# Pooled keys of the first batch on TensorE, and 768 instead of 1408 columns of zeros

## The chip, the cores and the metric

One core of a Trainium2 chip. The metric is the device time of one execution in microseconds. A core has five engines that run beside each other: TensorE (PE; its weight loads are listed as PEld), VectorE (DVE), ScalarE (ACT), GpSimd (POOL) and SyncE (SP), which issues the transfers (DMA).

## The reference, cut to what matters

The input is q, k and v of 2 batches, 8 heads, 576 positions and 64 elements a head, in f32. Two attentions are added. One is local (a position sees those nearer than 4), the other pooled: q, k and v are averaged over groups of 4 positions, attended over 144 positions, and each row of the result is repeated 4 times.

```
q_d = q.reshape(B, H, Sd, 4, D).mean(axis=3)      # k_d, v_d alike
out_up = np.repeat(sm_attn(q_d, k_d, v_d), 4, axis=2)
out_local = softmax(where(|i - j| < 4, scale * q k^T, -1e9)) v
x = out_up + out_local                            # to (1152, 512)
h = max(x @ w_in, 0);  x = (s * h * h + b) @ w_out         # 512 -> 2048 -> 512
out = sum over e of p[:, e] * (max(x @ w1[e], 0) @ w2[e])  # 4 experts, 512 -> 1024 -> 512
```

## The kernel before, in words

The attention comes in 16 units: four groups (a batch, and the first or second half of its positions) of four pairs of heads. Units 0 to 3 and 8 to 11 are first halves; only these load k and the pooled v of their pair, and the second half uses what they left. Eight loop steps (`steps`) take a unit through `a_step` (L484: k and q are transposed on TensorE and copied out by ScalarE), `k_step` (L534: on GpSimd, the transposed keys kT are added in groups of four, with two additions, tk and kd), `b_step` (L551: mask, local scores, pooled scores from kd, maxima and exponentials), `norm_step`, `c_step` (p is transposed), `d_step` (products with v), `x_step` and `v_step` (pooled v, on GpSimd). A loop turn i gives each step the unit i minus the step's lag, so the units overlap.

A planner orders the instructions of each engine by their priority and its own estimate of time; `a_step` and `b_step` of the first four units have a raised priority. GpSimd alone keeps the order in which the loop writes it. Every engine then runs its list in order. SP issues all the loads of q, k, v and weights in one list.

Matmuls on a tile of zeros (`idle`) fill TensorE's list: eight of 512 columns at the start, and at five places of a unit. `keep_warm` (L358) takes the free columns of the bank that the place has just written, and repeats a matmul of so many columns until the number in `fill` is reached; in `b_step` there are `fill // 448` of them ahead of the scores. `fill` is 1408 for units 0 to 3, 512 for units 4 to 9 and 0 after. ScalarE's copy out of a bank waits for the filler in it.

From loop turn 2 the weights of the first layer are prepared: they are split in a high and a low f32 part by ScalarE (L157, L196) and VectorE (L161 to L199). Partial products of the first layer (`ahead_products`, L761) start in the attention; they hold banks of the pool `psm`, which has three, and open a bank with one matmul on zeros (L771). After the attention come the rest of the first layer and the experts.

Of the kernel before, what the change touches and what calls it, by code (L numbers as in the profile page):

```python
# [8 lines left out]
F32 = mybir.dt.float32  # L9
# [3 lines left out]
ACTF = mybir.ActivationFunctionType  # L13
ALU = mybir.AluOpType
# [8 lines left out]
def attn_moe_moe_kernel(  # L23
# [14 lines left out]
    nc = tc.nc  # L38
# [4 lines left out]
    P = 128  # L43
# [7 lines left out]
    FAC = 4  # L51
    SD = S // FAC
    ND = SD // 2
    KP = 96
    KR = S // KP
    NP = H // 2
# [3 lines left out]
    scale = 1.0 / float(D) ** 0.5  # L60
    NEG = -8.0e9

    const = ctx.enter_context(tc.tile_pool(name="const", bufs=1))
# [5 lines left out]
    psm = ctx.enter_context(tc.tile_pool(name="psm", bufs=3, space=bass.MemoryType.PSUM))  # L69
# [255 lines left out]
        nc.vector.tensor_copy(identb[:, a], ident[:TQ, :TQ])  # L325

    mask = const.tile([TQ, MX + 2, W], BF16, name="mask")

    def make_mask(t, m):
        if t == 0:  # L330
            nc.gpsimd.memset(mask, 0.0)
        off = t * TQ - window(t) if t <= MX else S - TQ - window(NTQ - 1)
        for sgn in (1, -1):
            nc.gpsimd.affine_select(
                out=mask[:, t : t + m],
                in_=mask[:, t : t + m],
                compare_op=ALU.is_ge,
                fill=NEG,
                base=FAC - 1 + sgn * off,
                pattern=[[0, m], [-sgn, W]],  # L340
                channel_multiplier=sgn,
            )
# [15 lines left out]
    def keep_warm(ps, c0, cols):  # L358
        n = 512 - c0
        for _ in range(-(-cols // n) if n > 64 else 0):  # L360
            nc.tensor.matmul(ps[:, c0:], idle[:, :P], idle[:, :n], start=True, stop=True)  # L361
# [20 lines left out]
    NU = NG * NP  # L382
    actx = ExitStack()
    ap1 = actx.enter_context(tc.tile_pool(name="att1", bufs=1))
# [3 lines left out]
    psa = actx.enter_context(tc.tile_pool(name="psa", bufs=5, space=bass.MemoryType.PSUM))  # L388
    loaded = {}
    st = {}  # L390
    fill = [1408 if u < NP else 512 if u < 2 * NP + 2 else 0 for u in range(NU)]
    sums = [const.tile([P, MX + 2, 1], F32, name=f"sum{i}") for i in range(2)]

    GB = CUT * TQ // FAC
# [3 lines left out]
    def unit(u):  # L398
        g, j = divmod(u, NP)
        b, hf = divmod(g, HALVES)  # L400
        return g, j, b, hf

    def tiles(hf):

        return (0, CUT) if hf == 0 else (CUT, NTQ - CUT)
# [6 lines left out]
    def bank():  # L412
        return psa.tile([P, 512], F32, tag="a", name="psa")
# [70 lines left out]
    def a_step(u):  # L484
        g, j, b, hf = unit(u)
        if hf == 0:
            kn = loaded.pop(("k", u))
            kT = ap1.tile([P, S], F32, tag=f"kT{j}", name=f"kT{j}")
            view = kT.rearrange("p (n r) -> p n r", r=KR)
            m = KR // 2  # L490
            for c in range(2):
                psk = bank()
                for i in range(m):
                    last_pe["att"] = nc.tensor.transpose(
                        psk[:, i * KP : i * KP + KP],
                        kn[:, c * m + i].rearrange("p a d -> p (a d)"),
                        ident[:KP, :KP],
                    )
                keep_warm(psk, m * KP, fill[u])
                nc.scalar.activation(  # L500
                    out=view[:, :, c * m : c * m + m],
                    in_=psk[:, : m * KP].rearrange("p (t n) -> p n t", n=KP),
                    func=ACTF.Copy,
                    scale=scale / (FAC * FAC),
                )
            st["kT", j] = kT
        qn = loaded.pop(("q", u))
        n0, m = tiles(hf)
        gd = m * TQ // FAC
        psq = bank()  # L510
        for r in range(FAC):
            last_pe["att"] = nc.tensor.transpose(  # L512
                psq[:, r * gd : r * gd + gd],
                qn[:gd, r].rearrange("p a d -> p (a d)"),
                ident[:gd, :gd],
            )
        keep_warm(psq, m * TQ, fill[u])
        qz = ap2.tile([P, MX * TQ], F32, tag="qz", name="qz")[:, : m * TQ]
        nc.scalar.activation(
            out=qz.rearrange("p (t n r) -> p t n r", t=m, r=FAC),  # L520
            in_=psq[:, : m * TQ].rearrange("p (r t n) -> p t n r", r=FAC, t=m),
            func=ACTF.Copy,
            scale=float(FAC * FAC),
        )
        qd = ap2.tile([P, MX * TQ // FAC], F32, tag="qd", name="qd")[:, :gd]
        nc.vector.tensor_reduce(
            out=qd,
            in_=psq[:, : m * TQ].rearrange("p (r n) -> p n r", r=FAC),
            axis=AX.X,
            op=ALU.add,  # L530
        )
        st["q", u] = qz, qd

    def k_step(u):  # L534
        g, j, b, hf = unit(u)
        if hf == 0:
            kv = st["kT", j].rearrange("p (n r) -> p n r", r=FAC)
            t = ap4.tile([P, SD, 2], F32, tag="tk", name="tk")
            nc.gpsimd.tensor_tensor(out=t, in0=kv[:, :, :2], in1=kv[:, :, 2:], op=ALU.add)
            kd = ap1.tile([P, SD], F32, tag=f"kd{j}", name=f"kd{j}")  # L540
            nc.gpsimd.tensor_tensor(out=kd, in0=t[:, :, 0], in1=t[:, :, 1], op=ALU.add)
            st["kd", j] = kd
# [458 lines left out]
    def side_step():  # L1001
# [15 lines left out]
    steps = [  # L1017
        (b_step, 1),
        (a_step, 0),
        (k_step, 0),  # L1020
        (d_step, 3),
        (c_step, 2),
# [7 lines left out]
    for i in range(last + 1):  # L1030
# [13 lines left out]
        for f, lag in steps:  # L1044
            u = i - lag
            if 0 <= u < NU:

                with tc.high_priority(ahead.get(f, 0)) if f in ahead and u < NP else nullcontext():
                    f(u)
            if f is x_step and u >= 0 and u % NP == NP - 1:  # L1050
                slots += l1_steps(0, u // NP) + l2_steps(0, u // NP)
                firsts.append(slots[-FC - KD])
                if u < NP:

                    for _ in range(3):
                        take_slot()
            if f is norm_step:
                for g, (wait, n_fc) in AHEAD.items():
                    for kk in range(KD - 1):
                        if g * NP + kk + 3 + wait <= i < g * NP + NP + 3:  # L1060
                            for fc in range(n_fc):
                                if (0, 0, fc // 2) in ready:
                                    ahead_products(g, kk, fc)
            if f in (k_step, c_step) and slots and i < last:
                take_slot()
            if f in (b_step, k_step, c_step, v_step):
                side_step()
            if 5 <= i <= 7 and f in (d_step, norm_step):
                side_step()
# [112 lines left out]
```

## Time and profile before

| | us |
|---|---|
| median of 3 runs | 683.9 (683.66 to 684.03) |
| the profiled execution | 683.63 |
| its span | 681.9 |
| TensorE busy | 673.8 |
| VectorE busy | 403.9 |
| ScalarE busy | 344.5 |
| GpSimd busy | 104.2 |

Busy times are sums over the span; what bounds a stage is read from the chain of waits and from tables of that stage. The records of matmuls overlap in time, as they are pipelined: the chain gives how far one after another moves the work on, a line's mean the length of one record.

### The profile page before, as it was taken

How to read it: one execution, taken by the hardware profiler on the slowest of the kernel's cores; microseconds unless marked ns; L12 is line 12 of the kernel's file. 1: busy time of each engine (PE TensorE's matmuls, PEld its weight loads, DVE VectorE, ACT ScalarE, POOL GpSimd, SP SyncE). 2: the span in 40 equal slices, each digit the busy share in tenths (PEclk: the TensorE clock that was granted, in tenths of full speed). 3: DMA queues.
4: the chain of work that ended last, by engine and by line, in shares of the span. 5: the costliest groups of instructions: out<-in, count | busy, mean ns of one | idle time of the engine just before them, and what ended most of it. 6: DMA issues, size and time to landing. Idle time of an engine off the chain costs nothing.

```text
span 681.9 us, 11959 instructions
## 1 busy us (share of the span) xinstructions
PE 673.8 (99%) x4790; PEld 614.2 (90%) x4790; DVE 403.9 (59%) x720; ACT 344.5 (51%) x846; POOL 104.2 (15%) x123
## 2 busy tenths in 40 slices
PE   9999999999999999999999999999999999999997
PEld 6778888999999999999999898898998999989996
DVE  2899867798934325695435645546456365455442
ACT  3778688788856657754544333334234233333320
POOL 4431541100002001021201200211112012010000
PEclk9999999999999999999999999999999999999999
DMA  9986944234400001000301201111102012110012
GB/s 185 221 187 121 151 125 134 77 124 135 176 0 1 32 1 62 1 32 1 93 3 61 62 31 45 50 32 62 31 32 67 28 38 86 31 33 31 1 62 77
DMA packets 54167, 46.43 MB, mean 68 GB/s; under 512 B 32224, under 2 KB 42720, under 8 KB 54112
## 3 DMA queue, kind: packets, MB, share of 16 engines
q1 hardware_dynamic: 54112, 45.67, 25.3%
q8 instruction: 37, 0.61, 0.4%
q14 instruction: 18, 0.15, 0.1%
HBM read 43.31 MB, written 2.36 MB: 67 GB/s over the span
## 4 chain that ended last, share of the span: by engine, by line
PE 87%; DVE 7%; ACT 4%; POOL 1%; issue 1%; POOLq 0%; ACTq 0%; DVEq 0%
PE psm L316 40%; PE psx L902 26%; PE psx L316 13%; PE psa L361 2%; ACT pl L571 1%; PE psa L591 1%; PE psa L657 1%; PE psm L775 1%; PE psa L512 1%; DVE pl L632 1%; DVE cv L186 1%; DVE cv L175 1%; PE psa L685 0%; DVE cv L161 0%; DVE h L812 0%
## 5 line engine op out<-in xcount | busy, mean ns | idle before, releaser
L316 PE MATMUL psm<-w,h 128*128 128x512 f32 x864 | 208.7, 391 | 0.0
L316 PEld LDWEIGHTS psm<-w,h 128*128 128x128 f32 x864 | 158.5, 188 | 30.0
L902 PE MATMUL psx<-x,w 128*128 128x320 f32 (+1 forms) x768 | 117.8, 296 | 0.0
L902 PEld LDWEIGHTS psx<-x,w 128*128 128x128 f32 x768 | 109.3, 190 | 1.7
L259 POOL TENSOR_TENSOR sw<-raw 128x256 f32<-128x256 f32 x32 | 31.1, 992 | 413.2 <-DMA raw<-in_moe_w_dram 292.5
L917 ACT COPY r<-psx 128x320 f32<-128x320 f32 (+1 forms) x96 | 38.0, 396 | 92.4 <-PE psx L902 92.1
L920 ACT ACTIVATE h<-r 128x320 fp32r<-128x320 f32 (+1 forms) x96 | 42.0, 443 | 83.6 <-DVE r L931 83.6
L973 DVE SCALAR_TENSOR_TENSOR acc<-psm,pr,acc 128x512 f32<-128x512 f32 x63 | 47.2, 749 | 57.3 <-PE psm L316 57.3
L902 PE MATMUL psx<-t,w 128*128 128x320 f32 (+1 forms) x448 | 80.3, 302 | 0.2 <-DVE r L931 0.2
L931 DVE TENSOR_TENSOR r<-psx,r 128x320 f32<-128x320 f32 (+1 forms) x96 | 43.2, 456 | 58.6 <-PE psx L902 56.7
L902 PEld LDWEIGHTS psx<-t,w 128*128 128x128 f32 x448 | 67.0, 189 | 4.5 <-DVE r L931 0.5
L921 DVE SCALAR_TENSOR_TENSOR h<-r,h 128x320 fp32r<-128x320 f32 (+1 forms) x96 | 48.1, 506 | 18.5 <-ACT h L920 16.2
L316 PE MATMUL psm<-x,w 128*128 128x384 f32 (+2 forms) x348 | 56.8, 313 | 0.0
L316 PE MATMUL psm<-h,w 128*128 128x256 f32 (+2 forms) x360 | 56.4, 305 | 0.2 <-DVE h L812 0.2
L316 PE MATMUL psx<-h,w 128*128 128x384 f32 (+1 forms) x312 | 55.8, 327 | 0.0
L316 PEld LDWEIGHTS psm<-x,w 128*128 128x128 f32 x348 | 53.0, 189 | 0.4 <-ACT pT L660 0.2
L316 PEld LDWEIGHTS psm<-h,w 128*128 128x128 f32 x360 | 50.9, 190 | 1.3 <-DVE h L812 0.4
L316 PEld LDWEIGHTS psx<-h,w 128*128 128x128 f32 x312 | 52.0, 188 | 0.0
L316 PE MATMUL psx<-x,w 128*128 128x384 f32 (+2 forms) x252 | 43.1, 320 | 0.0
L316 PEld LDWEIGHTS psx<-x,w 128*128 128x128 f32 x252 | 40.6, 188 | 0.0
L237 DVE TENSOR_TENSOR w<-raw,w 128x1024 fp32r<-128x1024 f32 x16 | 19.5, 1224 | 26.2 <-ACT w L234 26.2
L819 DVE TENSOR_TENSOR h<-r,h 128x384 fp32r<-128x384 f32 (+2 forms) x40 | 21.6, 541 | 20.3 <-ACT h L818 19.1
(109 smaller groups left out, 888.2 us busy)
## 6 DMA issues: line engine op xcount, KB each, us to landing
raw<-in_moe_w_dram SPq DMA_DIRECT2D x32, 512.0 KB
raw<-in_moe_w_in_dram SPq DMA_DIRECT2D x8, 1024.0 KB
raw<-in_moe_w_out_dram SPq DMA_DIRECT2D x8, 1024.0 KB
kn<-in_k_dram SPq DMA_DIRECT2D x8, 288.0 KB
v<-in_v_dram SPq DMA_DIRECT2D x8, 288.0 KB
out_dram<-acc SPq DMA_DIRECT2D x9, 256.0 KB
qn<-in_q_dram SPq DMA_DIRECT2D x8, 160.0 KB
vn<-in_v_dram SPq DMA_DIRECT2D x16, 72.0 KB
```

Source lines behind the costliest of these rows:

```text
L175: nc.vector.scalar_tensor_tensor(out=c, in0=words()[0], scalar=29, in1=c, op0=ALU.logical_shift_right, op1=ALU.bitwise_or,)
L237: nc.vector.tensor_tensor(out=k0[1], in0=source(), in1=f32(k0[0]), op=ALU.subtract)
L259: nc.gpsimd.tensor_tensor(out=operand(out), in0=operand(x), in1=operand(y), op=op)
L316: nc.tensor.matmul(o, stat(ps, kk), mov(pm, kk, i), start=c == 0, stop=c == len(terms) - 1)
L361: nc.tensor.matmul(ps[:, c0:], idle[:, :P], idle[:, :n], start=True, stop=True)
L819: nc.vector.tensor_tensor(out=h[1], in0=r, in1=f32(h[0]), op=ALU.subtract)
L902: nc.tensor.matmul(ps, s_ap(n, half, a, w, kk), xt[x, pi][b][:, kk], start=first and c == 0, stop=c == len(terms) - 1, skip_group_check=True,)
L917: nc.scalar.copy(t, st[name])
L920: nc.scalar.activation(out=h[0][:, halves[hf]], in_=t, func=ACTF.Relu)
L921: nc.vector.scalar_tensor_tensor(out=h[1][:, halves[hf]], in0=t, scalar=0.0, in1=f32(h[0][:, halves[hf]]), op0=ALU.max, op1=ALU.subtract,)
L931: nc.vector.tensor_tensor(out=st[t], in0=st[name], in1=st[t], op=ALU.add)
L973: nc.vector.scalar_tensor_tensor(out=a, in0=ps, scalar=p_e, in1=a, op0=ALU.mult, op1=ALU.add)
```

## The change

A constant `pick` of 96 partitions by 6 times 144 columns is built at the start by GpSimd (a memset to one and two selections): column c of slice r is one where position 6p + r lies in group c of four. In units 0 to 3 (`u < NP`), `a_step` multiplies the six slices of the loaded keys with it on TensorE, into one bank of `psm`, and ScalarE copies the sum out as kd, with the scale that kT has. `k_step` then does nothing for these units; units 8 to 11 keep it. The filler of units 0 to 3 goes from 1408 to 768.

```
+    pick = const.tile([KP, KR, SD], F32, name="pick")
+    nc.gpsimd.memset(pick, 1.0)
+    for base, sgn in ((0, 1), (FAC - 1, -1)):
+        nc.gpsimd.affine_select(
+            out=pick,
+            in_=pick,
+            compare_op=ALU.is_ge,
+            fill=0.0,
+            base=base,
+            pattern=[[sgn, KR], [-sgn * FAC, SD]],
+            channel_multiplier=sgn * KR,
+        )
-    fill = [1408 if u < NP else 512 if u < 2 * NP + 2 else 0 for u in range(NU)]
+    fill = [768 if u < NP else 512 if u < 2 * NP + 2 else 0 for u in range(NU)]
             st["kT", j] = kT
+            if u < NP:
+                psd = psm.tile([P, 512], F32, tag="m", name="psm")[:, :SD]
+                for r in range(KR):
+                    nc.tensor.matmul(
+                        psd,
+                        kn[:, r].rearrange("p a d -> p (a d)"),
+                        pick[:, r],
+                        start=r == 0,
+                        stop=r == KR - 1,
+                    )
+                kd = ap1.tile([P, SD], F32, tag=f"kd{j}", name=f"kd{j}")
+                nc.scalar.activation(
+                    out=kd, in_=psd, func=ACTF.Copy, scale=scale / (FAC * FAC)
+                )
+                st["kd", j] = kd
-        if hf == 0:
+        if hf == 0 and u >= NP:
```

## Rows read from the trace of the kernel before

**Rows 1.** The page, busy time and share of the span, by engine.
```profile
PE 673.8 (99%) x4790; PEld 614.2 (90%) x4790; DVE 403.9 (59%) x720; ACT 344.5 (51%) x846; POOL 104.2 (15%) x123
```

**Rows 2.** The chain of waits, first 24 us: start us, us, what.
```profile
1.19 3.60 PE psa L361 x8
4.79 0.52 PE psm L771 x2
5.31 0.25 PE psa L494 x3
5.56 0.67 PE psa L361 x7
...
7.48 0.47 PE psa L584 x3
...
12.16 0.29 PE psa L604 x4
...
18.30 0.76 PE psa L361 x6
...
22.23 0.39 PE psa L604 x4
```

**Rows 3.** Table by stage: busy us (count) by engine, clock, DMA share, GB/s.
```profile
0.00:5.00 5.00, 3.81 (x10) 1.41 (x11) 0.61 (x5) 1.28 (x1) 2.26 (x11) 1.00 0.56 113
...
18.00:24.00 6.00, 6.00 (x66) 4.81 (x65) 5.90 (x12) 3.81 (x16) 2.28 (x4) 1.00 1.01 238
24.00:36.00 12.00, 11.32 (x159) 9.07 (x157) 10.92 (x19) 8.84 (x32) 5.01 (x6) 1.00 0.97 204
64.00:74.00 10.00, 10.00 (x131) 8.53 (x131) 9.79 (x18) 8.53 (x34) 3.87 (x3) 1.00 1.14 154
```

**Rows 4.** TensorE's waits after 140 us, all: total us, times, longest.
```profile
PE psx L902 <- DVE r L931: 0.2, 1, 0.2
```

**Rows 5.** Groups of instructions, first 30 us: count, busy us, mean ns of one.
```profile
L494 PEld LDWEIGHTS psa<-ident,kn 96*128 96x128 f32 x24 | 2.9, 141 | 0.5 <-issue 0.4
...
L604 PE MATMUL psa<-kd,qd 64*64 64x144 f32 x16 | 1.8, 297 | 0.0
L541 POOL TENSOR_TENSOR kd<-tk 128x144 f32<-128x144 f32 x4 | 1.8, 448 | 0.3
...
L571 ACT ACTIVATE pd<-psa,md 128x144 f32<-128x144 f32 x3 | 1.2, 387 | 0.0
...
L334 POOL TENSOR_SCALAR_AFFINE_SELECT mask<-mask 64x72 bf16<-64x72 bf16 x4 | 1.0, 238 | 0.1
...
L334 POOL TENSOR_SCALAR_AFFINE_SELECT mask<-mask 64x216 bf16<-64x216 bf16 x2 | 0.8, 396 | 0.0
...
L331 POOL MEMSET mask<- 64x504 bf16 x1 | 0.5, 515 | 0.0
```

**Rows 6.** Instructions in order of time, 17 to 37 us: start us, us, what.
```profile
17.27 1.13 ACT L157 ACTIVATE cv<-raw 128x1024 f32<-128x1024 f32 x1
...
21.53 1.22 DVE L186 SCALAR_TENSOR_TENSOR cv<-raw,cv 128x1024 int32<-128x1024 int32 x1
...
22.68 0.46 DVE L615 TENSOR_REDUCE ml<-psa 128x4 f32<-128x288 f32 x1
...
26.78 0.67 POOL L539 TENSOR_TENSOR tk<-kT 128x288 f32<-128x288 f32 x1 [1.98 <-ACT kT L500]
26.82 0.94 DVE L632 TENSOR_TENSOR pl<-pl,sum 128x288 f32<-128x288 f32 x1
...
27.43 0.58 ACT L660 COPY pT<-psa 72x512 f32<-72x512 f32 x1 [0.21 <-PE psa L657]
...
28.46 0.40 ACT L713 CAST x<-xg 128x256 fp32r<-128x256 f32 x1 [0.45 <-DVE xg L701]
...
36.07 0.46 DVE L632 TENSOR_TENSOR pl<-pl,sum 128x288 f32<-128x288 f32 x1
```

**Rows 7.** Waits of the first 30 us, GpSimd's for a transfer: total us, times, longest.
```profile
POOL v L474 <- DMA v<-in_v_dram: 3.6, 1, 3.6
```

**Rows 8.** Instructions in order of time, GpSimd's first masks: start us, us, what.
```profile
1.68 1.15 POOL L334 TENSOR_SCALAR_AFFINE_SELECT mask<-mask 64x72 bf16<-64x72 bf16 x4
```

## The prediction, made before the change ran

> **What bounds the kernel now.** I read the page first. TensorE is busy for 99% of the span [rows 1]. A matmul's end is modelled there, and part of this work is filler on zeros, so the share alone does not say that TensorE sets the time; three views by stage do.
>
> The chain of waits over the first 24 us runs through TensorE without a break, and through its filler too: the two 512-column matmuls on zeros at 4.79, the seven after the first transposes of k at 5.56, the three ahead of the scores at 7.48 [rows 2]. Here a filler matmul taken away can move the end. The table by stage shows the next one: from 18 to 24 us VectorE is busy 5.90 of 6.00, from 24 to 36 us 10.92 of 12.00, from 64 to 74 us 9.79 of 10.00, while TensorE's busy time still holds filler [rows 3]. There VectorE, preparing the weights of the first expert layer, is the limit, and a shorter TensorE gives nothing. After 140 us the list of waits has one entry for TensorE, 0.2 us [rows 4]: what is won or lost before reaches the end whole. So the question is by how much VectorE's full block, which starts when ScalarE takes up the first weights at 17.27 [rows 6], moves, and whether something inside it gets longer or shorter.
>
> **The change part by part.** The four units of the first batch that load k (units 0 to 3) get less filler and six new matmuls each, and lose two GpSimd additions.
>
> *Filler.* The places round their count up. A tile of transposed k has 224 free columns, 1408 needs seven matmuls and 768 four; the q tile has 256, six become three; ahead of the scores three become one; behind the transposes of p six become three; behind the output eight become four. That is 18 matmuls a unit. Prices: 0.67/7 = 0.096 us for 224 columns, 0.76/6 = 0.127 for the 256 (the row holds the fill with its lead), 0.47/3 = 0.157 ahead of the scores [rows 2].
>
> *New matmuls.* Six a unit, 96 rows, 144 columns, f32. The trace of before has none on the whole array. The nearest is the pooled scores: 144 columns on a quarter of the array; 16 records for the eight matmuls of four units, so an f32 matmul leaves two records [rows 5]. Six make 12 records. Four of the pooled records take 0.29 us in the chain [rows 2], two side by side, so 0.145 us a step: 12 x 0.145 = 1.74 us a unit. By the transposes of k, 0.25/3 = 0.083 for 96 columns [rows 2], 144 columns are 0.125, and a unit 1.50. The bounds are wider: one pooled record by itself, 0.29/4 = 0.073, gives 0.87; a weight load of 0.141 [rows 5] that hides behind nothing, plus 0.125, gives 3.2. I take 1.6, between the two nearest rows. [...]
>
> *Step 1, up to ScalarE's first weights at 17.27.* Ahead of it on TensorE lie the k transposes of units 0 to 2, and q and scores of units 0 and 1. Taken away: 18 x 0.096 = 1.72, 6 x 0.127 = 0.76, 4 x 0.157 = 0.63. Also the two matmuls on zeros at 4.79 leave this stretch, 0.52: they open a bank of the three-bank pool from which the new sums now take theirs first, so they must wait for one. Together 3.6. Added: units 0 and 1, 2 x 1.6 = 3.2 (unit 2's come behind its transposes). Net -0.4, bounds -1.9 to +2.8. It counts only if the weights have landed by then, which no row shows (ScalarE goes from kT straight on to them).
>
> *Step 2, up to the scores of unit 2.* Away: q fill of unit 2 0.38, scores 0.31, one k tile of unit 3 0.29, together 1.0; added: unit 2, 1.6; so +0.6. The pooled scores of unit 2 end at 22.23 + 0.39 = 22.62 [rows 2]; VectorE's reduction of them starts at 22.68, and the preparation step ahead of it, begun at 21.53, ends at 22.75 [rows 6]. The slack is 0.13 us. With VectorE's block 0.4 earlier and the scores 0.2 later than now, VectorE waits 0.5, and steps 1 and 2 together are +0.1 us (bounds -1.9 to +4.9, the second with three units at 3.2). VectorE is strict in its order here, so the maxima, the normalisation and the second weight step all stand behind this wait.
>
> *Step 3, GpSimd freed.* Four times 0.67 and 0.45 us [rows 5, 6]. GpSimd is no bound here, it idles for 3.6 us on a DMA [rows 7]. But while its addition for unit 3 runs from 26.78, VectorE's multiplication at 26.82 takes 0.94 us, and the same shape takes 0.46 at 36.07 [rows 6]; this is inside VectorE's full block. Gain 0.48, bounds 0 to 0.7 (the third unit's additions overlap two reductions that are no longer than elsewhere).
>
> *Step 4, a copy more on ScalarE.* 128x144 out of PSUM; the exponential of that shape takes 0.387 [rows 5], a plain copy rather 0.3. For units 0 to 2 ScalarE has room (3.81 busy of 6.00 [rows 3]). Unit 3's falls near 26.5, where ScalarE idles 0.21 ahead of 27.43 and 0.45 ahead of 28.46 [rows 6]; it takes those. Without that cover the copy of p and all behind it is 0.3 late. I take +0.1, bounds 0 to 0.4.
>
> *Costed at nothing.* The new constant: a memset of 864 columns at 0.515/504 is 0.88, two selections at 0.238 + 792 x 0.0011 (from the rows of 72 and 216 columns) 1.11 each [rows 5], together 3.1 us on a GpSimd that is done with its first masks at 2.83 [rows 8]. Even with the masks ahead of it the constant is there at 5.9. TensorE asks for it after two tiles of transposes with their filler, at 5.31 + 2 x 0.25 + 8 x 0.096 = 6.6, or at 6.1 if the two matmuls at 4.79 are gone [rows 2]; the mask is wanted just ahead of 7.48. The cover is 0.2 us at the least; beyond it, each us late is one us on TensorE. The k buffers come free later by the new matmuls, and SP's in-order queue would pass that on to the loads behind, but the DMA engines are full there anyway (share 1.01 from 18 to 24 us [rows 3]), so the queue has stock. The fill behind p and output in units 1 to 3 falls after 23 us, where TensorE does not bound.
>
> *Sum.* +0.1 - 0.48 + 0.1 = -0.3 us on the profiled execution's 683.63 (span 681.9 and 1.7 around it): 683.3. The median of the three runs is 683.9, 0.3 higher, so 683.6 against that; I give 683.4. Less than about 0.2% (1.4 us) cannot be told from no change here.
>
> **The rivals.** *A, TensorE's filler was the real cost.* For it: the unbroken chain of rows 2. Up to 23.4 us some 24 x 0.096 + 9 x 0.127 + 6 x 0.157 + 0.33 + 0.52 = 5.2 us of filler go. If the new matmuls run at the transposes' record, 0.083, whatever their columns, four units cost 4.0; VectorE's block comes 1.2 earlier, with 0.48 of step 3 and half of its 1.08 idle us from 24 to 36 [rows 3] filled: -2.2, 681.4. Against: it needs the first weights landed 1.2 us earlier, while the DMA engines are full.
>
> *B, the new matmuls stretch the path (the other side).* Place: TensorE ahead of the scores of unit 2. At 0.20 us a record (load and multiplication half hidden) a unit costs 2.4, three units 7.2 against the 4.6 of filler taken away there: +2.6, less 0.5 of step 3, 685.7. It breaks even at 0.141 us a record (36 of them cost 5.1, the filler and step 3 give 4.6 + 0.5) and decides from 0.18, where 1.4 us are lost. For it: 0.141 us of weight load in each record. Against: loads overlap elsewhere, as the transposes at 0.083 show.
>
> [...]
>
> *D, it does not do what it says.* The pooled keys were nowhere waited for and the first weights land late: nothing moves but the 0.48, inside the forecast's band.
>
> **How the numbers follow.** Forecast with D 0.42: 683.4, own range 682.5 to 684.8. A 0.33. B 0.17, C 0.06, and 0.02 for a constant that comes late. A lies below -0.2%, B and C at or above +0.2%: faster 0.33, same 0.42, slower 0.25. The range 681.3 to 685.7 reaches to A's and B's values and leaves about a fifth outside, the far bounds of steps 1 and 2 among it.
>
> **What would show it.** Step 1: ScalarE's first weight step at 16.9 to 17.3. The new records: 0.125 to 0.145 us each, 12 a unit. Step 2: VectorE waiting for TensorE up to half a us ahead of unit 2's reduction. Step 3: the multiplication at about 26.5 back at 0.46. Step 4: ScalarE's new copy near 0.3 us. A first weight step before 16.3 means A; new records above 0.18 us, or scores of unit 2 that end later than 24, mean B; idle-column matmuls at twice their time after 5 us mean C. The forecast is wrong if the stage after 140 us changes its length, or if the order of the instructions on VectorE in the weight preparation is another one.

## The result, and the profile after

| | us |
|---|---|
| before, 6 runs beside it | 683.96 median (683.66 to 684.87) |
| after, 6 runs | 689.29 median (688.09 to 692.95) |
| ratio | 1.0078 [1.0067, 1.0089] |
| profiled execution of after, span | 688.09, 686.3 |

The change costs 5.3 us by the medians, 4.5 by the profiled executions. It was forecast to change nothing (683.4), and the time lies outside the range. The page's busy line answers to [rows 1]:

```profile
PE 676.6 (99%) x4766; PEld 617.0 (90%) x4766; DVE 406.4 (59%) x720; ACT 345.1 (50%) x850; POOL 101.3 (15%) x118
```

The chain of waits of after, first 24 us (start us, us, what), beside [rows 2]:

```profile
4.93 0.44 PE psa L506 x3
5.37 0.39 PE psa L373 x4
...
6.39 1.49 PE psm L522 x12
...
12.44 1.18 PE psm L522 x8
...
17.38 1.02 ACT cv L157
...
21.64 2.21 DVE cv L186
```

The new sums (L522) take 12 records in 1.49 us, the thinner filler four in 0.39, and ScalarE is at the first weights at the same time as before. So far the sizes are as forecast. Where the time goes is seen by the starts of the local scores of a unit, the first row "psa<-kT,qz" of each in TensorE's timeline (us):

| kernel | unit 3 | 4 | 6 | 7 | 8 | 11 | 15 |
|---|---|---|---|---|---|---|---|
| before | 28.13 | 35.35 | 50.03 | 57.94 | 69.14 | 90.34 | 116.70 |
| after | 29.23 | 34.97 | 52.70 | 60.62 | 73.86 | 94.45 | 120.82 |

After is 0.4 ahead at unit 4, loses 3.05 from unit 4 to 6 and 2.04 from 7 to 8, and gets 0.6 back. The lead of 0.4 at unit 4 is TensorE's alone: VectorE is 1.56 us late there, as place 1 shows. The loss of 4.1 at unit 15 stays to the end; past 140 us TensorE's waits are still 0.2 in all [rows 4]. TensorE's waits from 20 to 140 us in after (total, times, longest), the two long ones first:

```profile
PE psm L802 <- ACT acc L859: 1.6, 1, 1.6
PE psm L802 <- ACT w L196: 1.4, 1, 1.4
```

*Place 1, units 4 to 6.* VectorE's timeline of before (start us, us, engine line op):

```profile
36.66 1.22 DVE L199 TENSOR_TENSOR w<-cv,w 128x1024 fp32r<-128x1024 f32 x1
37.80 0.53 DVE L615 TENSOR_REDUCE ml<-psa 128x5 f32<-128x360 f32 x1
...
45.61 1.22 DVE L199 TENSOR_TENSOR w<-cv,w 128x1024 fp32r<-128x1024 f32 x1
```

and of after:

```profile
38.21 0.53 DVE L642 TENSOR_REDUCE ml<-psa 128x5 f32<-128x360 f32 x1
38.65 0.51 DVE L644 TENSOR_REDUCE md<-psa 80x1 f32<-80x144 f32 x2
39.08 1.21 DVE L199 TENSOR_TENSOR w<-cv,w 128x1024 fp32r<-128x1024 f32 x1
...
49.61 1.21 DVE L199 TENSOR_TENSOR w<-cv,w 128x1024 fp32r<-128x1024 f32 x1
50.74 0.48 DVE L553 TENSOR_REDUCE qd<-psa 128x80 f32<-128x320 f32 x1
```

The step that makes the second weights (L199) stood ahead of the maxima of unit 4 and now stands behind them; so does the third behind unit 5's. It ends 2.4 and 4.0 us later. The new place is only 0.87 us of the 2.4 (the two maxima): VectorE was already late ahead of it. TensorE, in its timeline of after, waits for the high part of those weights. ScalarE makes it (L196) as soon as VectorE's L186 has ended, which is at 36.94 in after and 35.38 before, 1.56 us late. So this wait comes from VectorE's lateness up to there and TensorE's small lead, not from where L199 stands. TensorE's timeline of after, ScalarE's, and VectorE's L186 of before and of after:

```profile
38.06 0.69 PE L802 MATMUL psm<-x,w 128*128 128x256 f32 x3 [1.41 <-ACT w L196]
39.18 2.17 PE L802 MATMUL psm<-x,w 128*128 128x256 f32 x8 [0.42 <-POOL x L742]
```
```profile
36.97 1.04 ACT L196 CAST w<-cv 128x1024 fp32r<-128x1024 f32 x1 [2.63 <-DVE cv L186]
```
```profile
34.17 1.21 DVE L186 SCALAR_TENSOR_TENSOR cv<-raw,cv 128x1024 int32<-128x1024 int32 x1
```
```profile
35.73 1.21 DVE L186 SCALAR_TENSOR_TENSOR cv<-raw,cv 128x1024 int32<-128x1024 int32 x1
```

Behind the first of these holes, at 38.8, its clock falls. The table by stage (36 to 46 us; clock is the third number from the right), before and then after:

```profile
36.00:46.00 10.00, 9.48 (x118) 7.52 (x114) 9.86 (x18) 7.14 (x24) 4.43 (x3) 1.00 0.75 167
```
```profile
36.00:46.00 10.00, 8.17 (x61) 6.76 (x60) 9.31 (x16) 5.85 (x20) 4.08 (x3) 0.66 0.63 156
```

*Place 2, units 7 to 8.* ScalarE's timeline of before has two copies of the first expert's sums (acc) ahead of the exponentials of a unit (L571):

```profile
63.89 0.88 ACT L832 COPY acc<-psm 128x256 f32<-128x256 f32 x2
64.67 0.33 ACT L571 ACTIVATE pl<-psa,ml 128x72 f32<-128x72 f32 x1
```

in after one; the next two stand behind all of them (L598), and a bank that TensorE wants is held until then. ScalarE's timeline, then TensorE's:

```profile
66.95 0.36 ACT L859 COPY acc<-psm 128x256 f32<-128x256 f32 x1
67.19 0.34 ACT L598 ACTIVATE pl<-psa,ml 128x72 f32<-128x72 f32 x1
...
69.39 0.65 ACT L859 COPY acc<-psm 128x256 f32<-128x256 f32 x2
```
```profile
69.83 0.56 PE L802 MATMUL psm<-x,w 128*128 128x320 f32 x2 [1.62 <-ACT acc L859]
```

None of the instructions that changed places is part of the change. The planner wrote them in another order.

### The profile page after: what moved, and what is told of

Read it like the earlier page. It is cut to its first block, busy times and chain, and to the rows that moved or that the text cites. A ratio compares the mean times of both kernels' runs of the same rounds, so it can differ in the third digit from the quotient of the medians.

```text
span 686.3 us, 11905 instructions
## 1 busy us (share of the span) xinstructions
PE 676.6 (99%) x4766; PEld 617.0 (90%) x4766; DVE 406.4 (59%) x720; ACT 345.1 (50%) x850; POOL 101.3 (15%) x118
## 4 chain that ended last, share of the span: by engine, by line
PE 91%; DVE 5%; ACT 2%; issue 1%; POOL 1%; POOLq 0%; ACTq 0%
PE psm L316 41%; PE psx L929 26%; PE psx L316 13%; PE psa L373 2%; PE psm L802 2%; PE psa L684 1%; PE psa L618 1%; PE psa L712 1%; PE psa L539 1%; PE psa L705 1%; DVE cv L186 1%; PE psa L506 1%; PE psm L522 1%; DVE cv L175 1%; PE psa L641 0%
## 5 line engine op out<-in xcount | busy, mean ns | idle before, releaser
L948 DVE SCALAR_TENSOR_TENSOR h<-r,h 128x320 fp32r<-128x320 f32 (+1 forms) x96 | 49.7, 522 | 18.5 <-ACT h L947 16.4
```

The source lines that it names most:

```text
L948: nc.vector.scalar_tensor_tensor(out=h[1][:, halves[hf]], in0=t, scalar=0.0, in1=f32(h[0][:, halves[hf]]), op0=ALU.max, op1=ALU.subtract,)
```

## The experiments

Two kinds of edit are used. In the one, the finished lists of after or before are kept on every engine, and only matmuls on zeros (or sums) of TensorE's list are taken out or copied (`_edit`); so the order of everything else stays. In the other, the text is changed and the planner orders anew. The theories: C, the clock falls behind TensorE's waits and that is the loss; S, TensorE's time in units 0 to 3 (the sums) makes all else late; O, the planner's other order of VectorE and ScalarE costs the time. In the table below, starts are as above, ratios to before with 95% interval. The starts come from one profiled execution, which need not be a typical one: it was the fastest run of after (688.09), before_1344 (686.09), acc_first and after_640, the slowest of gap_filled (692.98), all_covered and fill_undone, and the second slowest of after_896 (687.39).

| kernel | order | median us (range) | ratio | unit 3 | 4 | 6 | 7 | 8 | 15 |
|---|---|---|---|---|---|---|---|---|---|
| before_thinned | before's | 683.2 (682.45 to 685.51) | 0.9992 [0.9982, 1.0003] | 26.29 | 33.65 | 49.13 | 57.03 | 68.21 | 115.80 |
| thinned_covered | before's | 684.01 (683.16 to 686.01) | 1.0002 [0.9992, 1.0012] | 26.68 | 34.03 | 49.62 | 57.53 | 68.72 | 116.27 |
| gap_filled | after's | 691.07 (689.2 to 692.98) | 1.0099 [1.008, 1.0117] | 29.83 | 35.56 | 52.50 | 60.37 | 75.80 | 125.65 |
| after_thick | after's | 693.82 (693.02 to 694.48) | 1.0147 [1.0132, 1.0163] | 35.01 | 41.69 | 57.43 | 65.29 | 78.55 | 125.97 |
| few_sums | after's | 688.62 (685.95 to 693.09) | 1.0076 [1.0042, 1.011] | 32.09 | 37.83 | 54.77 | 62.63 | 75.89 | 123.31 |
| all_covered | after's | 688.2 (687.07 to 690.54) | 1.0063 [1.004, 1.0086] | 29.10 | 34.83 | 51.77 | 62.60 | 75.85 | 123.25 |
| few_sums_covered | after's | 690.84 (686.79 to 691.83) | 1.0089 [1.0056, 1.0121] | 27.35 | 33.09 | 51.51 | 59.42 | 75.03 | 123.11 |
| after_thinned | after's | 689.33 (687.56 to 697.16) | 1.0116 [1.0055, 1.0177] | 28.35 | 34.58 | 51.60 | 59.52 | 72.79 | 120.22 |
| thin_alone | new | 688.18 (686.93 to 689.34) | 1.0061 [1.0043, 1.0078] | 23.87 | 34.27 | 52.71 | 62.00 | 74.21 | 121.38 |
| before_1344 | new | 688.11 (686.09 to 688.28) | 1.0047 [1.003, 1.0065] | 27.49 | 34.63 | 49.44 | 58.02 | 71.29 | 119.21 |
| fill_undone | new | 693.71 (693.08 to 695.58) | 1.0144 [1.0125, 1.0162] | 38.70 | 45.44 | 59.34 | 68.84 | 78.45 | 128.28 |
| acc_first | after's to 66 us | 688.62 (687.38 to 688.69) | 1.0061 [1.0046, 1.0076] | 28.81 | 34.54 | 52.23 | 60.15 | 71.47 | 119.60 |
| after_640 | new | 687.38 (685.67 to 692.38) | 1.0062 [1.0033, 1.0091] | 28.91 | 35.58 | 49.85 | 59.10 | 71.44 | 118.51 |
| after_784 | new | 690.27 (688.79 to 691.3) | 1.009 [1.0074, 1.0106] | 30.18 | 36.23 | 50.97 | 59.57 | 74.46 | 122.82 |
| after_896 | new | 685.51 (684.56 to 687.41) | 1.0024 [1.0015, 1.0034] | 33.12 | 38.99 | 53.52 | 61.44 | 72.62 | 120.20 |

**gap_filled.** Six copies of the 512-column matmul on zeros into TensorE's hole at 36.7.

```
+    banks = [v for (_, line), v in _fillers(nc).items() if line == 798]
+    load, mm = banks[1][0]
+    _edit(nc, behind={mm.name: (load, mm, 6)})
```

> The changed kernel with the order of all engines as it is, and six more matmuls on zeros (512 columns) put into TensorE's list behind the bank opening at 36.3 us, where it waits 1.4 us for the weights and its granted clock then reads 0.50 from 39 to 45.4 us. Theory (the clock): the clock stays at 1.00, the work from 39 to 45 us takes some 3 us less, and the end comes 2 to 3 us earlier than the changed kernel's 689.3: 686.3 to 687.3, ratio to before about 1.004. Rival (the clock's loss lies off the path, VectorE sets the pace there): the clock stays at 1.00 and the time is within 0.5 us of 689.3. Rival (filler costs): slower by the 1.3 us put in.

The clock held from 36 to 70 us, yet unit 6 began at 52.50, hardly before after's 52.70: TensorE now waits 1.42 us for VectorE's qd, which stands behind the third L199, as in before, in a list that is 2.9 us late there (50.55, before 47.62). Behind the next hole, the one for acc, the clock fell instead (0.54 from 70 to 80 us). Table by stage, then TensorE's timeline:

```profile
36.00:46.00 10.00, 9.12 (x99) 6.56 (x97) 9.62 (x17) 6.38 (x22) 4.09 (x3) 1.00 0.67 161
...
70.00:80.00 10.00, 10.00 (x86) 8.10 (x86) 7.25 (x14) 4.46 (x8) 0.86 (x1) 0.54 1.10 157
```
```profile
51.08 0.30 PE L684 MATMUL psa<-ident,pl 128*72 128x128 f32 x1 [1.42 <-DVE qd L553]
```

So the fall of the clock in place 1 is not the whole of what makes unit 6 late; VectorE is late without it. The time, 691.07, is none of the three expected: 1.8 above after. The second fall of the clock comes on top of the zeros put in, priced at 1.3, so the run does not price either.

**before_thinned, after_thick.** The zeros alone, in either direction: 72 matmuls (those between 768 and 1408) taken out of before, or put into after.

```
+    thin = {(361, 7): 4, (361, 6): 3, (361, 8): 4, (584, 3): 1}     # in before
+    _edit(nc, take=take)
+    thick = {(224, 4): 3, (256, 3): 3, (192, 4): 4, (288, 1): 2}     # in after
+    _edit(nc, behind=behind)
```

> The kernel before with its order as it is, and only the filler of the first four units thinned to the counts of the change (72 matmuls on zeros taken out of TensorE's list; nothing else moved). Theory (the clock): TensorE's waits from 28 to 38 us grow by the filler taken away, the clock falls to half in that stretch as it does in the changed kernel, and the time is 1.5 to 3 us above before. Rival (filler was on the path up to 23 us): 1 to 2.5 us below before. Rival (filler is off the path and the clock holds): within 0.7 us of before.

> The changed kernel with its order as it is, and the filler of the first four units back at the counts of before (72 matmuls on zeros put in). Theory (the clock, and TensorE on the path up to 30 us): the clock holds at 1.00 and gives back 2 to 3 us, but 4 to 5 us of filler now lie ahead of unit 3's scores at 29.2, so these come at 32 to 34 and the time is 690 to 692. Rival (thin filler is the whole loss): 684 to 685. Rival (filler hidden by waits in the changed order): clock back, 686.3 to 687.3.

In before's order the zeros are worth nothing: units 3 and 4 come 1.7 to 1.8 us earlier, and the end can't be told from before's. With the sums on TensorE they bind: the same zeros make unit 3 5.8 us later and cost 4.5 of the median, 1.8 more than the highest time expected.

**few_sums.** Sixteen of the 24 matmuls of the sums left out (the pooled keys of the first batch are incomplete).

```
+    take += [(ins,) for ins in block.instructions if ... ins.debug.lineno == 522
+             and not ins.start_tensor_calc and not ins.stop_tensor_calc ...]
+    _edit(nc, take=take)
```

> The changed kernel with its order as it is, and of the six new matmuls of each of the units 0 to 3 only the first and the last left (the pooled keys then sum two slices of six: part of the computation is left out). Each unit's new work falls from some 1.5 to 0.5 us. Theory (the new matmuls are a small part of the loss; order and clock the rest): the scores of unit 3 come 0.5 to 1.5 us earlier than 29.2, the gap at 36.7 stays and with it the clock at half, 687.5 to 689. Rival (the price of the new matmuls is the loss): 3 to 4 us less than the changed kernel, 685 to 686. Rival (idle grows and the clock falls earlier): above 689.5.

Inconclusive, for a reason of its own: TensorE idled 0.50 us at 4.9, and the rows behind ran at about half rate until about 16 us (three transposes of k with four fillers of 224 columns take 1.26 us from start to start, in after 0.66; the four fillers 0.95 us, in after 0.55 at 5.21), though the table's clock reads 1.00 there. TensorE's timeline, then the table:

```profile
5.36 0.71 PE L506 MATMUL psa<-ident,kn 96*128 96x96 f32 x3 [0.50 <-POOL mask L346]
5.87 0.95 PE L373 MATMUL psa<-idle 128*128 128x224 bf16 x4
6.62 0.69 PE L506 MATMUL psa<-ident,kn 96*128 96x96 f32 x3
...
10.20 0.95 PE L373 MATMUL psa<-idle 128*128 128x224 bf16 x4
```
```profile
5.00:15.00 10.00, 9.64 (x45) 7.21 (x47) 0.32 (x1) 2.44 (x6) 2.95 (x8) 1.00 1.25 200
```

Before had the two 512-column matmuls at 4.79 [rows 2] in that place. With the sums in the banks, they come at 30.6 and 36.3.

**all_covered.** After, with two matmuls on zeros more at the opening, six at 36.7, eleven at 68.2.

```
+    behind = {opening: (load, mm, 2), banks[1][0][1].name: (*banks[1][0], 6),
+              third.name: (load, mm, 11, third)}    # zeros added to an open sum
+    _edit(nc, behind=behind)
```

> The changed kernel with the same order of instructions on every engine, and three more groups of matmuls on zeros in TensorE's order: 2 of 512 columns behind the opening ones (4.65 us), 6 of 512 where the scores of unit 4 end (36.7), 11 of 320 where it waits at 68.2 for the acc copy. Theory O (the new order of the instructions on VectorE and ScalarE costs the time, the granted clock next to nothing): in gap_filled the clock stayed at 1.00 up to 60 us and the scores of unit 6 still began at 52.50 (after: 52.70), since VectorE was late there; so the clock is 1.00 all the way to 140 us, unit 6 begins at about 52.2, units 7 to 8 still take 13.2, and the time is 687.3 to 688.7. Theory C (the falls of the clock behind TensorE's waits are the loss): 684.5 to 685.5. In both the runs lie within 1.5 us of each other, if the hole at the opening made the spread of 688.1 to 693.0.

Three runs at a granted clock of 0.999 or more took 687.07, 687.80 and 688.61 us; the profiled one, 690.54, had its fall behind the 1.42 us wait for qd, from some 52.2 to 58.9 us (granted clock 0.66 from 50 to 60 us). With the clock up, after's order, with the sums in it, still costs some 3 to 4.5 us over 684.08. That decides against C as the larger part, by the mean clocks of three runs that left no trace. It does not part the order from the time of the sums. The spread did not shrink as expected.

**few_sums_covered, after_thinned.** few_sums, or after with 28 zeros fewer, the opening covered by three matmuls on zeros.

```
+    _edit(nc, take=take, behind={opening: (load, mm, 3)})
```

> The changed kernel with its order, without the four middle ones of the six matmuls of each pooled sum (so the pooled keys of the first batch are incomplete: 16 matmuls, about 4 us of TensorE's time, are left out), and with 3 matmuls on zeros of 512 columns behind the opening ones, so that TensorE doesn't idle at 4.9 us as it did in few_sums. Theory S (the sums' time on TensorE in the first four units makes VectorE's steps late, and those the later units): unit 3 begins near 26.5 instead of 29.23, VectorE doesn't wait at 30.2, unit 6 begins near 50.5 instead of 52.70, and the time is 685.5 to 686.5 (the acc copies still cost 1.9 behind unit 7). Theory O (the order on VectorE, whatever TensorE's lead): unit 3 early, unit 6 at 52 or later, 687.5 to 688.5.

> The changed kernel with its order, 28 of the matmuls on zeros of the first units left out (0.10 to 0.12 us each, 2.9 us in all) and the opening covered by 3 of 512 columns. Theory S: as few_sums_covered, a little less: unit 3 near 27.5, unit 6 near 51.3, 686.3 to 687.5. Theory O: unit 6 at 52 or later, 687.5 to 689. A third (the clock wants the zeros): the granted clock falls inside the first four units, unit 3 no earlier than 29, 689 or more.

S as the whole falls. Unit 4 begins 1.9 us earlier than in after without the sums, and 0.4 without the zeros, and neither reaches the end: 690.84 and 689.33. VectorE's order takes the lead from unit 1 on: in few_sums_covered the scores of unit 1 begin at 16.06 (after 17.43), but its maxima stand behind L161, which waits for ScalarE, and begin at 18.78 (after 19.03). What is left of the lead turns into a longer wait for the same weights (1.73 us in few_sums_covered) and the clock falls behind it (0.66 from 36 to 46 us). Both medians lie above what O expected too. That the sums cost nothing is not shown: the one run of few_sums_covered at a clock of 0.995 took 686.79, near S's range; the other three, at 0.989, 690.47 to 691.83.

**thinned_covered.** before_thinned with ten matmuls on zeros in the two waits ahead of its fall (granted clock 0.50 from 38 to 40 us).

```
+    _edit(nc, take=take, behind={ahead.name: (load, mm, 6, last[0]), last[2].name: (load, mm, 4, last[0])})
```

> The kernel before with its order, the zeros of the first four units thinned as in before_thinned (72 matmuls out), and 6 plus 4 matmuls on zeros of 256 columns in the two waits of TensorE at 34.9 and 36.6 us, behind which before_thinned had a clock of 0.50. Theory C: the scores of unit 5 begin at 42.3 instead of 43.80, and the lead of 1.7 us of unit 4 lasts: 681.7 to 682.5, ratio about 0.997. Theory O (VectorE is what is late behind unit 5): the clock stays at 1.00 but unit 6 begins at 48.8 or later (before_thinned 49.13), 682.8 to 683.4.

Clock 1.00 throughout, unit 5 at 42.94 (42.3 expected), unit 6 only 0.4 ahead of before: VectorE takes the lead back. The median, 684.01, is above both ranges: no gain.

**thin_alone, before_1344, fill_undone.** One number of the text, the order planned anew.

```
-    fill = [1408 if u < NP ...           # in before
+    fill = [768 if u < NP ...            # thin_alone; 1344 in before_1344
-    fill = [768 if u < NP ...            # in after
+    fill = [1408 if u < NP ...           # fill_undone
```

> The kernel before with 768 columns of zeros a place in the first four units instead of 1408, its order planned anew: one part of the change alone. With before's order kept, the same zeros left out gave 683.2 and 684.0 (before_thinned, thinned_covered). Theory S: TensorE leads by 1.7 us at unit 3, VectorE takes it back by unit 6: 682.5 to 684.5, no change. Theory O: a draw of the planner, in which an acc copy stands behind the exponentials again (one of three here, against two of three in after): 684.5 to 687.

> The kernel before with 1344 columns of zeros a place in the first four units instead of 1408, nothing else: the same 18 idle matmuls a unit are a little narrower or one fewer, some 0.5 us of TensorE in all. Its order is planned anew: two of the first three acc copies of ScalarE stand behind the exponentials, as in after, and VectorE's third weight step (L199) stands behind the maxes of unit 5. Theory O: 685.5 to 687.0, with a wait of TensorE for acc near 68 us and 13 us between units 7 and 8. Rival (what the change computes costs the time, not the order): 683.4 to 684.2.

> The changed kernel with 1408 columns of zeros a place in the first four units again; the order of the instructions is planned anew. With the order of after kept, the same zeros cost 4.5 us (after_thick 693.8). Theory O (order): ScalarE's and VectorE's orders differ from after's, and the time is another draw: it may come out anywhere from 685 to 691, and is told by whether the acc copies stand ahead of the exponentials (units 7 to 8 in 11.2 or 13.2 us). Rival (the sums on TensorE themselves are the loss, 1.5 us a unit on its path): 690 or more whatever the order.

before_1344 differs from before by twelve matmuls on zeros, three in each of the four units (eight of 224 columns and four of 192, about 1.1 us), and by its order. It keeps step with before to unit 7 (58.02, before 57.94), then loses 2.0 us at place 2, clock 1.00 in all of it. ScalarE's and TensorE's timelines of before_1344:

```profile
64.31 0.38 ACT L832 COPY acc<-psm 128x256 f32<-128x256 f32 x1
64.58 0.33 ACT L571 ACTIVATE pl<-psa,ml 128x72 f32<-128x72 f32 x1
...
66.82 0.65 ACT L832 COPY acc<-psm 128x256 f32<-128x256 f32 x2
```
```profile
67.25 0.41 PE L775 MATMUL psm<-x,w 128*128 128x320 f32 x1 [1.58 <-ACT acc L832]
```

That is O with before's computation: 1.0047. The profiled execution shows 2.0 us of it; the other three runs, 688.00 to 688.28 at a clock of 0.998, are 2 us longer than it, above the range expected, and for them there is no trace. thin_alone costs 4.2 us, above both ranges, where the same 72 zeros left out in before's order (before_thinned) cost nothing: the same instructions in two orders. fill_undone missed O's range; it came out at after_thick's time with an order of its own, which speaks for the sums and the full zeros binding TensorE together, as S says of that case.

**acc_first.** The acc copies with a higher priority; the order is after's up to 66 us.

```
+            with tc.high_priority(60):
                 nc.scalar.copy(a, ps)
```

> The changed kernel with a higher priority for ScalarE's copies of the first expert's sums (acc, L859): the order of every engine is that of after up to 66 us, then two of the three copies pass the exponentials of a unit. Theory O: the wait of 1.62 us at 69.83 goes, units 7 to 8 take 11.5 instead of 13.24, and the time is 687.0 to 688.0 (about 1.6 under after's median of 689.3). Rival (the ten exponentials are as urgent, they only change places): units 7 to 8 take 12.5 or more, 688.5 to 689.5. Rival C: a gain above 2 us with a clock of 1.00 where after has its fall.

Units 7 to 8 take 11.32 instead of 13.24: place 2 is what it was said to be. The gain by the median is only 0.7 us, so the time expected was missed: units 8 to 11 lose 0.7 again (21.31 us against 20.59), the order behind is new too, and unit 12 to 13 takes 7.55 us (7.11 in after).

**after_640, after_784, after_896.** Other fills in after, taken for the order that they bring: in all three the second L199 stands ahead of the maxima, as in before; in after_896 two acc copies also stand ahead of the exponentials.

```
-    fill = [768 if u < NP ...
+    fill = [640 if u < NP ...            # 784, 896
```

> The changed kernel with 640 columns of zeros a place instead of 768. In its order VectorE's second L199 stands ahead of the maxes of its unit, as in before and unlike after; the acc copies stand behind the exponentials, as in after. Theory O: TensorE doesn't wait 1.4 us for w at 36.7, unit 6 begins by 51.0, units 7 to 8 take 13.2, and the time is 685.5 to 687.5. Rival (sums): 688 or more.

> The changed kernel with 784 columns of zeros a place instead of 768: 8 idle matmuls of 256 columns more (about 0.9 us of TensorE), and an order in which VectorE's second weight step (L199) stands ahead of the maxes of its unit, as in before; the acc copies stand as in after. Theory O: no wait of 1.4 us for w at 36.7, so the clock stays at 1.00 up to 60 us, unit 6 begins at 51 to 52, units 7 to 8 take 13.2, and the time is 686.0 to 688.0. Rival (TensorE's time): 690.

> The changed kernel with 896 columns of zeros a place: in its order the second L199 stands ahead of the maxes and both acc copies ahead of the exponentials, as in before; only the third L199 stands as in after. Theory O: units 7 to 8 take 11.2, TensorE's time in the first four units is paid once (unit 3 near 32) and not given back: 685.5 to 687.5. Rival (TensorE's time decides): 690 or more.

Units 4 to 6 take 14.27, 14.74 and 14.53 us (before 14.68, after 17.73): the loss of place 1 is gone in all three. In after_896 that is in part because TensorE is late and no longer leads: after_thick, in after's order with unit 4 at 41.69, takes 15.74. Units 7 to 8 take 12.34, 14.89 and 11.18: place 2 is gone only in after_896, ScalarE's timeline there:

```profile
67.39 0.87 ACT L859 COPY acc<-psm 128x256 f32<-128x256 f32 x2
68.16 0.33 ACT L598 ACTIVATE pl<-psa,ml 128x72 f32<-128x72 f32 x1
```

after_896 is the best of the changed kernels, though TensorE has more zeros in it than in after and unit 3 begins 3.9 later. Its 1.0024 [1.0015, 1.0034], 1.7 us, is what is left when both places stand as in before; after lost 5.3. after_784 missed its expectation and came out at the rival's time (690.27): the clock fell behind its wait for acc. TensorE's timeline, then the table:

```profile
68.81 0.56 PE L802 MATMUL psm<-x,w 128*128 128x320 f32 x2 [1.62 <-ACT acc L859]
```
```profile
70.00:78.00 8.00, 8.00 (x78) 6.52 (x78) 5.81 (x12) 3.24 (x8) 0.86 (x1) 0.57 1.11 163
```

In after_640 two runs at a clock of 0.999 and 1.000 took 685.67 and 686.64, one at 0.997 686.39, the three at 0.991 to 0.995 688.13 to 692.38.

**acc_first_512, acc_first_640, acc_first_960.** acc_first with these fills (`fill = [512 if u < NP ...`, and so on).

> The changed kernel with the acc copies' higher priority and 512 columns of zeros a place in the first four units, planned anew: a candidate. Theory S: 256 columns fewer at some 20 places, 2.2 us less on TensorE by unit 3, on top of acc_first (688.6): 686 to 687.5. Theory O: a draw, 685 to 690. If the zeros of 768 are what keeps the clock up, it falls in the first 30 us and the time is above 689.

> after_640 with the acc copies' higher priority: both places stand as in before. Theory O: units 7 to 8 take 11.5, and the time is 684.0 to 685.8, the best of the changed kernels. Rival (sums): 687.5 or more.

> The changed kernel with the acc copies' priority and 960 columns of zeros: VectorE's second and third L199 both stand ahead of the maxes, two of three acc copies ahead of the exponentials; TensorE has some 1.7 us more of zeros up to unit 3 than after. Theory O: the 1.7 us are paid at unit 4 and not given back, but no more is lost: 685.5 to 687.5. Rival (the zeros on TensorE's path decide): between after and fill_undone, 690 to 692.

688.25, 689.33 and 687.65 us. The first is in O's range, which was wide. The second missed: TensorE waits 1.31 us for GpSimd and 1.05 for an acc copy, and the clock falls behind both (0.70 from 40 to 45 us, 0.53 from 70 to 75); its one run at a clock of 1.000 took 686.31, nearly the expected. The third has unit 3 at 34.28, 6.2 later than before, and is still 5.2 late at unit 15 (121.89) in its profiled execution, the slowest of the four. No version beats before: the two in its order with fewer zeros can't be told from it.

## Why the prediction was wrong, point by point

*Filler and new matmuls: right.* 0.39 us for four of 224 columns; 1.49 for the first twelve records (0.124 each), 0.148 and 0.128 for the next rows of eight and four. 1.6 a unit was taken.

*Step 1: right for the first weights only.* ScalarE's first weight step began at 17.26. But unit 1's local scores came 0.54 later (17.43, before 16.89): they wait for ScalarE's copy of q (qz), which now stands behind a copy of unit 2's keys (kT). ScalarE's timeline of before, then of after:

```profile
16.45 0.38 ACT L519 ACTIVATE qz<-psa 128x256 f32<-128x256 f32 x1 [0.64 <-PE psa L361]
16.93 0.47 ACT L500 ACTIVATE kT<-psa 128x288 f32<-128x288 f32 x1
```
```profile
16.66 0.47 ACT L512 ACTIVATE kT<-psa 128x288 f32<-128x288 f32 x1 [1.20 <-PE psa L373]
17.00 0.37 ACT L546 ACTIVATE qz<-psa 128x256 f32<-128x256 f32 x1
```

The two opening matmuls at 4.79, counted as 0.52 us gone, gained 0.38 (the transposes of k begin at 4.93, not 5.31) and covered the landing of k. Without them TensorE idles 0.42 us (after_640) to 0.66 (after_896) there in some runs, and in some of these, as few_sums and after_896, goes on at about half rate (0.95 us for the four fillers, in after 0.55).

*Step 2: too small, and the wait the other way round.* VectorE was to wait for unit 2's pooled scores; these waited 0.48 us for VectorE's qd, which stood ahead of L186 (21.13) and now stands behind it (23.77). Unit 2's local scores come 1.16 late (22.09, before 20.93) and unit 3 is 1.1 late, against +0.1 for steps 1 and 2. The price of the matmuls is not the main reason: with 16 of the 24 left out, unit 1's maxima still begin only 0.25 earlier (few_sums_covered, 18.78). VectorE now takes up L161, which waits for ScalarE, ahead of these maxima; before, they stood ahead of it. VectorE's timeline of before, then of after:

```profile
17.95 0.46 DVE L615 TENSOR_REDUCE ml<-psa 128x4 f32<-128x288 f32 x1 [0.65 <-PE psa L604]
...
18.54 0.68 DVE L161 TENSOR_SCALAR cv<-cv 128x1024 f32<-128x1024 f32 x1
```
```profile
18.42 0.69 DVE L161 TENSOR_SCALAR cv<-cv 128x1024 f32<-128x1024 f32 x1 [0.59 <-ACT cv L157]
19.03 0.45 DVE L642 TENSOR_REDUCE ml<-psa 128x4 f32<-128x288 f32 x1
```

The maxima are 1.08 late, and so is all that hangs on them.

*Step 3: right, and half of a sum.* The multiplication went to 0.46. But GpSimd, whose pooled v had landed by 21.49 (22.21 before), began ahead of VectorE's L186, which took 2.26 us where it took 1.22 in [rows 6]. VectorE's and GpSimd's timelines of after:

```profile
21.59 2.26 DVE L186 SCALAR_TENSOR_TENSOR cv<-raw,cv 128x1024 int32<-128x1024 int32 x1
...
27.70 0.46 DVE L659 TENSOR_TENSOR pl<-pl,sum 128x288 f32<-128x288 f32 x1
```
```profile
21.49 1.27 POOL L486 TENSOR_TENSOR v<-v 72x512 f32<-72x512 f32 x1 [7.68 <-DMA v<-in_v_dram]
```

In before, all_covered and acc_first GpSimd began behind L186, by 0.68, 0.23 and 0.82 us; there L186 took 1.22, and GpSimd's addition, 1.27 in after, took 1.67, 2.13 and 1.54. It is no large part of the loss: all_covered and acc_first, with L186 at 1.22, still lost (688.2 and 688.62).

*Step 4: right,* 0.29 to 0.31 us a copy. *The constant:* 0.82 and twice 0.94, no wait of size.

*The sum* of -0.3 is what stood at TensorE's unit 4, 34.97 against 35.35, but that is luck: unit 3 was 1.1 late, and units 3 to 4 took 5.74 us instead of 7.22, where steps 3 and 4 had 0.4 to give. *The step that failed* lies under all four: every list was taken to keep its order ("VectorE is strict in its order here"), and a new order had no term and no chance in the sum. It fails from unit 1 on, as step 2 shows, and costs most at places 1 and 2. The last line of the prediction named another order on VectorE as a sign of its being wrong, and ScalarE's was not thought of. The planner works from its own estimate of time, and a change of zeros alone (thin_alone, before_1344) moves orders far behind the edit. Place 1 cost 3.0 us and place 2 2.0 in the profiled execution. On VectorE the lateness at place 1 splits so: unit 6's qd is 3.12 late (50.74, before 47.62). Of that, 1.56 stood at the end of the second L186. From there to this qd before takes 12.24 us; gap_filled, all_covered and after_thick, in after's order with a clock of 1.00 in that stretch, take 13.02, so the order costs 0.78; after, with the clock down, takes 13.80, 0.78 more. How much of the first 1.56 is the sums' own time is not settled; 1.10 of it was there at unit 3's maxima.

*Rival C had 0.06* for a fall of the clock by the thinner filler, at a cost of 0.2% or more. The clock did fall, 0.50 in after from 38.8 to 45.6, but behind a hole in TensorE's list; with the thick filler of fill_undone it fell too (0.66 from 35 to 40 us). Not each hole brought a fall (1.00 behind 1.62 us at 69.83 in after), and one fall came without a hole (fill_undone's). No run shows by itself what a fall costs at the end: C's place above +0.2% was the author's estimate, and before_thinned, with thinner filler and 0.50 from 38 to 40 us in its profiled run, came out at 0.9992. By all_covered the clock is the smaller part of the loss: its runs with the clock up average 687.8, after's median is 689.3. It goes with part of the spread only: four runs of few_sums, all at a mean clock of 0.995, lie between 685.95 and 690.83. *Rival B*'s sign (scores of unit 2 ending past 24) appeared, without its cause: the records took 0.124, not 0.18. *Rival A* is answered by before_thinned: zeros taken away give TensorE 1.7 us and the kernel nothing that can be told from noise.

What stays open: a run of gap_filled at a mean clock of 1.000 took 690.91, 3 us above all_covered's; its opening is not covered, and half rate there doesn't show in that figure, but that is argued, not shown. The change with before's order on every engine was not tried, since the new instructions have no place in it.

## What to carry to other kernels

Where a planner orders the lists from estimated times, an edit is priced in two parts: the work itself, with the order held, and the new order, which must be read list by list, on engines that the edit doesn't touch as well. Look in each list for an instruction that waits for another engine and now stands ahead of one that a third engine is waiting for. An engine's lead was worth nothing here while a second one was full in the same stretch (before_thinned: unit 4 begins 1.70 us earlier, the time is 0.9992 of before's); it became a hole, and the clock fell behind some of the holes (to 0.50 in after).

## What the runs showed of the hardware

- TensorE's granted clock fell to 0.50 in after at 38.8 us, behind an idle stretch of 1.41 us and 0.7 us of work, just as a second stretch of 0.42 began. It stayed there to 45.6 us, from 39.18 on without a gap in TensorE's work. In all_covered it read 0.66 from 50 to 60 us, behind a single wait of 1.42 us that ended at 50.35, in the profiled run (mean clock 0.994); if it fell to 0.50, that is 6.8 us of the ten, an estimate, and the twenty local scores at 51.77 took 1.17 us where those at 34.83 took 0.85. Three other runs had 0.999 or more.
- Like holes did not always do this: the clock stayed at 1.00 behind the wait of 1.62 us at 69.83 in after and behind one of 1.30 us at 39.08 in after_640.
- In fill_undone it read 0.66 from 35 to 40 us (3.4 us at 0.50, by the same estimate; eight fillers of 192 columns took 1.42 us at 35.13, and 0.83 at 41.92), with no wait of TensorE on record from 25 to 45 us. Ahead of the fall, from 30.7 us on, TensorE's list was short matmuls one or two at a time.
- Behind an idle stretch of 0.50 us at the opening, the rows ran at about half rate until about 16 us in few_sums (1.26 us where after takes 0.66), while the table of the clock read 1.00. Behind 0.51 us at the same place in after_784 only the first three did (0.68 us; four fillers then took 0.56). So the hole alone does not decide it.
